# A linear-attention and feed-forward kernel: a table of engines and a new written-out order for its opening

## The chip, the cores and the metric

The kernel runs on one core of a Trainium2 chip. The metric is the device time of that core in microseconds (us). The core has a matrix engine (PE, whose weight loads are shown apart as PEld), a vector engine (DVE), a scalar engine (ACT), a general engine (POOL) and SP, whose queue issues nearly all transfers here.

## The reference

Attention over a small memory is followed by a feed-forward layer. Cut to what matters:

```python
# q, k, v: (8, 8, 576, 64); phi: (8, 8, 576, 32)
a = softmax(phi, axis=2)                       # over the 576 positions
k_m, v_m = a^T k, a^T v                        # 32 rows for each head
attn = softmax(q k_m^T / 8, axis=-1)           # over 32
x = (attn v_m), heads side by side             # (4608, 512)
h = x @ w_in                                   # w_in (512, 2048)
out = (h - tanh(h)) @ w_out                    # w_out (2048, 512)
```

## The kernel before

Every matrix operand is split into a high and a low f16 part, so one product is two or three products of f16. The weights arrive as 64-bit floats. They are loaded in 32 tiles of 512 KB, i0 to i15 of `w_in` and o0 to o15 of `w_out`. Two tiles make a pair, p = 0 to 15 (pairs 8 to 15 are of `w_out`). A pair is turned into f16 in steps: the upper bits are cast into `tops`, then joined with the lower words to f32 in `wq` or `wt`, then scaled and rounded to the high part `win_hi` or `wout_hi`, and what is left becomes `win_lo` or `wout_lo`.

The rows fall into 18 units of 256; a batch b has 576 rows, so a unit can span two batches. The hidden dimension falls into four blocks fb. For a batch, the logits `pt` are loaded and their maximum `mx` is taken, they go through the exponential, and PE turns them (`pet`, `pel`) into `e`. PE then pools keys and values with them (`pkv`), DVE normalizes the result (`kr`, `kvn`), and PE turns it (`ptr`) into `kT` and the value parts `vh`, `vl`. Scores `psc` are made for each half t of the rows; their softmax runs in place in `sc` (maximum `sm`, subtraction, exponential, sum `sz`, division), and the turned result `af` is split into `ah` and `al`. For each block, the pooled values times `w_in` (`pp`) are split into `ph` and `pl`. A first product `h` of `ah`, `al` with `ph`, `pl`, a polynomial on ACT and DVE (`u`, `h`, `g`) and a second product `o` with `w_out` finish a unit.

Units 4 to 17 run in a regular loop. Everything before it is the opening: some 180 us whose order stands as a written-out list of words, `START`. Each word advances one step by one piece: `FX0` loads the logits of batch 0, `KA0` and `KB0` its keys and values, `i4:kv2` two weight tiles into a buffer, `Q00` a half of its queries, `V00` and `V01` are the pooling, `N0` the normalization, `U0` and `UV0` the turn, `S00` the scores of half 0, `AM`, `AE`, `AD`, `AT`, `AS` the softmax and split of a half, `T01` a pair's conversion, `Lp00` its low part through PE, `P00` and `PL00` a block's `pp` with its high and its low part, `H10` the first product of unit 1 and block 0, `a` and `ap` the polynomial, `M00` the second product. `Z00` is two warming products (`warm`), whose result nobody reads. After the list `in_order` ties every engine to the order in which its instructions were written. So an engine that waits holds up all that is written behind it. SP's transfers go through the same list, and an issue waits while eight transfers are under way.

The one psum buffer `pa` serves, one after the other, `psc` of half 0, every `pp` of the opening and, from batch 1 on, `pet`, `pkv` and `ptr`. Two buffers `h` serve the first products, the low parts through PE and part of batch 0. What the change touches are the steps `top_bias`, `expo_rows`, `expo_turn`, `soft_max`, `soft_div`, `conv`, `low`, `low_pool`, `att_split`, `g2_high`, `g3`, and `START`.

Of the kernel before, what the change touches and what calls it, by code (L numbers as in the profile page):

```python
# [20 lines left out]
P = 128  # L21
# [31 lines left out]
N_ROWS = 2  # L53
# [18 lines left out]
Z00 o11:pp5 Q11 N1 Tv10 U1 Tv08 U1 Tv10 H01 o8:gg T11 UV1 UV1 T11 T09 W0 a10 ap00 Tv08 Lv09 S10 S10 ap00 H11 Lv08 H01
Tv10 a10 ap01 AM10 c00 H11 S11 Tv10 M00 a11 a10 P10 AM10 i8:kv2 c10 S11 AE10 a11 L11 AMv11 KB2 AD10 M10 AMv11 P11 a11
i10:kv3 AD10 L11 P10 Th04 AT10 AE11 a11 FA2 FX2 P11 PL10 ap01 Lv10 cv11 AS10 AD11 PL11 ap01 o10:q AD11 Tv05 Tv05
i14:kv3 M11 AT11 Tv05 Th04 ap01 cv01 Th04 OP1 AS10 AS11 H20 H20 AS11 i12:kv2 o9:q H21 ap20 Tv05 M01 Th04 ap20 H21 Lv04
a21 X2 T07 Lv05 ap20 XP2 KA2 a21 a21 ap20 H31 H30 OP0 Y2 H30 P02 P02 T07 cv20 T07 H31 Tv12 a21 Y2 c21 Tv12 T13 M20
Tv06 V20 PL02 Q20 V21 H02 T07 a31 ap30 ap30 Lv07 a31 Tv12 ap30 a31 H12 P12 Tv12 Tv06 Tv06 M21 Tv06 N2 a31 Lv06 P12 H02
T13 ap02 ap30 c30 PL12 o14:kv3 ap02 ap02 OP2 P03 o12:kv2 M30 P03 PL03 H12 Q21 U2 H03 ap12 T13 H13 ap02 W1 ap12 UV2 U2
Tb14 T13 UV2 c02 ap12 ap12 H03 Tb14 S20 Tb14 a03 H22 c31 Tb15 P13 S20 H13 ap13 L12 c12 ap13 P13 Tb14 M31 AM20 FQ3 S21
ap13 PL13 X3 H22 a03 a03 OP3 Lv13 H23 AM20 AE20 P20 H23 a03 S21 KR30 ap13 G00 AMv21 a22 R1 a22 AMv21 L12 W2 AE21 M02  # L80
Tb15 Tb15 Tb15 cv13 a22 Lv14 Lv15 M12 a23 M13 P20 a23 P21 c03 AD20 a22 PL20 H32 a23 a23 P21 AD20 H32 H33 M03 O1 cv22
AT20 ADv21 G10 AS20 PL21 H33 ADv21 a32 O1 R0 M22 AS20 a32 ap33 ap33 O0 a32 a32 FA3 P22 cv23 H41 ap33 cv32 AT21 H40 G01
O0 G20 AS21 ap33 c33 H40 M23 P23 M32 H41 P22 ap40 G21 PL22 ap40 R2 O2 P23 ap41 O2 ap40 R3 ap40 AS21 ap41 ap41 M33 PL23
ap41 c40 G11 cv41 G30 O3 F40 O3 G31
"""
W_TAG = "qt us ot qt ot qt pr ot qt pr us ot qt us ot qt".split()
N_CHECK = N_F1 + 2 * B + DF // P + DM // P


class Attention:  # L90
# [172 lines left out]
    def turn(self, b, d, ps=None):  # L263
# [9 lines left out]
        nc.scalar.activation(d["kT"], pa[:, 0, 0:128], AF.Copy)  # L273
# [29 lines left out]
    def soft_max(self, b, d, t, eng=None):  # L303
# [12 lines left out]
    def soft_div(self, b, d, t, scale, eng=None):  # L316
# [7 lines left out]
        (eng or nc.gpsimd).tensor_tensor(s3, s3, z.unsqueeze(2).to_broadcast((P, NB, 32)), op=ALU.mult)  # L324
# [971 lines left out]
```

## Time and profile before

| | us |
|---|---|
| median of 3 runs (642.98 to 643.99) | 643.63 |
| span of the profiled execution | 640.4 |
| PE busy in it | 629.1 (98%) |
| DVE busy | 515.6 (81%) |
| ACT busy | 371.7 (58%) |
| POOL busy | 233.7 (36%) |

The span is that of the instructions of one profiled execution. The median of the timed runs lies 3.2 us above it. Warming products count as busy time of PE like any others.

### The profile page before, as it was taken

The numbers are of one execution on the slowest core, as the hardware profiler recorded it, in microseconds if no ns is written. First come the engines' busy times: TensorE is split into PE (matmuls) and PEld (weight loads), VectorE is DVE, ScalarE is ACT, GpSimd is POOL, SyncE is SP. The second block draws the span as 40 slices with busy tenths as digits, with TensorE's granted clock in tenths as the row PEclk, the third lists the DMA queues.
The fourth block names the chain that finished last, engine by engine and source line by source line (L and its number), as shares of the span: only waits on it lengthen the run. The fifth ranks groups of instructions, "written<-read, shape, count | busy, mean of one in ns | idle before, by whom it ended". The sixth has DMA issues, their size and how long they took to land.

```text
span 640.4 us, 15316 instructions
## 1 busy us (share of the span) xinstructions
PE 629.1 (98%) x6592; PEld 453.4 (71%) x6592; DVE 515.6 (81%) x757; ACT 371.7 (58%) x493; POOL 233.7 (36%) x155
## 2 busy tenths in 40 slices
PE   7899999999999999999999999999999999999997
PEld 3364665645667777787777787777788777888886
DVE  3989998979785777876898889878988888858765
ACT  2878588645424455545565465545565576676641
POOL 1306212511212244422534363434432565455430
PEclk9999999999999999999999999999999999999999
DMA  8994573233122402244313422441353334234200
GB/s 333 410 401 202 194 293 136 68 120 133 53 86 104 166 5 76 39 152 174 107 58 136 173 74 69 157 175 34 108 159 140 100 105 129 62 113 131 92 35 37
DMA packets 27723, 85.48 MB, mean 133 GB/s; under 512 B 3584, under 2 KB 4096, under 8 KB 26880
## 3 DMA queue, kind: packets, MB, share of 16 engines
q1 hardware_dynamic: 26496, 82.34, 37.0%
q10 hardware_dynamic: 1152, 2.10, 0.9%
q8 instruction: 53, 0.87, 0.6%
q14 instruction: 22, 0.18, 0.1%
HBM read 72.88 MB, written 11.54 MB: 132 GB/s over the span
## 4 chain that ended last, share of the span: by engine, by line
PE 72%; DVE 9%; issue 6%; ACT 5%; POOL 4%; DMA 3%; SPq 0%; POOLq 0%; ACTq 0%; DVEq 0%
PE hs L628 17%; PE x L773 12%; PE o L766 10%; PE o L709 8%; PE o L773 8%; PE h L628 6%; PE pp L580 3%; POOL g L664 2%; PE pkv L241 2%; DVE h L653 2%; DVE h L643 2%; DMA q<-in_qt_dram 2%; ACT u L635 2%; PE o1h L709 2%; DVE f L677 2%
## 5 line engine op out<-in xcount | busy, mean ns | idle before, releaser
L664 POOL TENSOR_TENSOR g<-h,g 128x1024 f16<-128x1024 f32 x63 | 137.2, 2178 | 330.9 <-ACT g L659 244.2
L628 PEld LDWEIGHTS <-ph 128*128 128x128 f16 x2304 | 177.6, 98 | 18.5 <-issue 4.7
L628 PE MATMUL hs<-ah,ph 128*128 128x256 f16 (+3 forms) x1152 | 151.4, 246 | 0.0
L659 ACT ACTIVATE g<-h 128x1024 f16<-128x1024 f32 x72 | 76.0, 1056 | 111.6 <-DVE h L653 103.2
L628 PE MATMUL hs<-al,ph 128*128 128x256 f16 (+3 forms) x576 | 127.6, 246 | 0.0
L643 DVE SCALAR_TENSOR_TENSOR h<-hs,u 128x1024 f32<-128x1024 f32 x54 | 65.8, 1219 | 72.5 <-ACT u L635 71.8
L648 ACT ACTIVATE u<-u,beta 128x1024 f32<-128x1024 f32 x72 | 82.5, 1147 | 65.2 <-DVE h L643 65.2
L766 PE MATMUL o<-wout_hi,g 128*128 128x512 f16 x432 | 104.6, 379 | 0.0
L773 PEld LDWEIGHTS <-f 128*128 128x128 f16 x896 | 87.7, 98 | 10.2
L653 DVE SCALAR_TENSOR_TENSOR h<-u,h 128x1024 f32<-128x1024 f32 x72 | 88.7, 1233 | 4.1 <-ACT u L648 3.1
L773 PEld LDWEIGHTS <-g 128*128 128x128 f16 x672 | 64.2, 98 | 27.3 <-issue 6.0
L773 PE MATMUL x<-bt,f 128*128 128x256 f16 x672 | 82.5, 273 | 0.0
L635 ACT ACTIVATE u<-hs 128x1024 f32<-128x1024 f32 x54 | 54.8, 1014 | 27.1 <-PE hs L628 24.4
L709 PEld LDWEIGHTS <-g 128*128 128x128 f16 x384 | 36.8, 98 | 46.6 <-issue 3.3
L677 DVE TENSOR_TENSOR f<-g 128x512 f16<-128x512 f16 x112 | 68.3, 650 | 1.7
L766 PEld LDWEIGHTS <-g 128*128 128x128 f16 x432 | 41.2, 98 | 40.2 <-issue 3.8
L709 PE MATMUL o<-wout_hi,g 128*128 128x512 f16 x192 | 58.8, 380 | 0.0
L628 PE MATMUL h<-ah,ph 128*128 128x256 f16 (+3 forms) x384 | 49.6, 246 | 0.0
L628 PE MATMUL h<-al,ph 128*128 128x256 f16 (+2 forms) x192 | 42.5, 246 | 0.0
L709 PE MATMUL o<-wout_lo,g 128*128 128x512 f16 x96 | 36.4, 379 | 0.0
L598 DVE SCALAR_TENSOR_TENSOR ph<-pp,ph 128x1024 f16<-128x1024 f32 x26 | 31.5, 1211 | 3.1 <-ACT ph L593 3.1
L495 POOL TENSOR_TENSOR fy<-chk 128x512 f32<-128x512 f32 x32 | 33.6, 1064 | 0.0
(164 smaller groups left out, 936.7 us busy)
## 6 DMA issues: line engine op xcount, KB each, us to landing
q<-in_qt_dram SPq DMA_DIRECT2D x16, 576.0 KB, 5.1
kv<-in_kva_dram SPq DMA_DIRECT2D x16, 516.0 KB, 6.9
chk<-in_w_in_dram SPq DMA_DIRECT2D x16, 512.0 KB, 6.1
chk<-in_w_out_dram SPq DMA_DIRECT2D x16, 512.0 KB, 3.4
out_dram<-r SPq DMA_DIRECT2D x28, 256.0 KB, 2.4
kv<-in_kva_dram SPq DMA_DIRECT2D x6, 1032.0 KB, 9.7
raws<-in_w_in_dram SPq DMA_DIRECT2D x12, 511.8 KB, 8.9
raw<-in_w_out_dram SPq DMA_DIRECT2D x12, 511.8 KB, 9.1
```

What stands on the lines that cost most here:

```text
L495: nc.gpsimd.tensor_tensor(y, hf, hf, op=ALU.mult)
L628: nc.tensor.matmul(hp[:, k, tu : tu + w], px[:, g, cs], d[ax][:, g, ta : ta + w], start=(n == 0), stop=(n == 5),)
L635: nc.scalar.activation(uu, hp, AF.Square, scale=1.0 / (S_A * S_P))
L643: nc.vector.scalar_tensor_tensor(h3, hp, C2 * S_G / (S_A * S_P), uu, op0=ALU.mult, op1=ALU.mult)
L648: nc.scalar.activation(uu, uu, AF.Square, bias=c["beta"])
L653: nc.vector.scalar_tensor_tensor(h3, uu, CC, hp, op0=ALU.add, op1=ALU.mult)
L659: nc.scalar.activation(gg[:, 0], h3, AF.Copy)
L664: eng.tensor_tensor(gg[:, 1], h3, gg[:, 0], op=ALU.subtract)
L677: nc.vector.tensor_tensor(o, x, y, op=op)
L709: nc.tensor.matmul(o, gx[:, k, P * tt : P * tt + P], wx[:, 4 * fb + k, :], start=(first and k == 0 and wx is wout_hi and gx is gh), stop=( ...
L766: nc.tensor.matmul(o[th], gg[:, 0, k, P * th : P * th + P], wout_hi[:, 4 * fb + k, :], start=(first and k == 0), stop=False)
L773: nc.tensor.matmul(dst, a(1 - n, kk), b(n, kk), start=(new and kk == 0 and n == 0), stop=(end and kk == 1 and n == 1))
```

## The change

Three things change. `START` is written anew: the logits of batch 0 are loaded first, the loads of the weight tiles come in another order and partly in other buffers, most of the warming products move, and the pieces are interleaved differently. A table `ENGINE_LIST` names the engine (v for DVE, g for POOL, otherwise ACT or the step's default) of each copy, scaling and difference, where before a letter in the word chose it. And the two rows of logits of a batch (`pt[:, 0]`, `pt[:, 1]`) go apart through maximum, exponential and turn.

```diff
-KB0 Z00 Z00 Z00 FX0 i4:kv2 X0 Z00 Z00 KA0 Z00 Z00 YX0 Z00 Z00 i0:pp4 Z00 Z00 Z00 XT0 XT0 Z00 V00 Tv02 Tv02 V01 Tv02 N0
+FX0 Z00 XR00 XR01 YX00 KA0 XT00 YX01 XT01 KB0 XT00 V00 XT01 XT01 Z00 V01 Z00 Z00 N0 U0 Z00 i4:kv2 Q00 T02 T02 UV0
...
+ENGINE_LIST = """
+g: hi1 hi12 lo1 lo10 lo12 lo13 lo14 lo4 lo5 lo6 sc6 tops12 tops14 tops6 tops9
+v: ah11 ah21 al01 al20 al21 div01 div21 e00 el0 el1 gh0_1 gh0_2 gh0_3 gh1_2 gh2_1 gh2_3 gh3_2 gh3_3 gl0_1 gl0_3 gl1_1
+v: gl1_2 gl2_0 gl2_2 gl4_1 hi15 hi2 hi4 hi7 kT2 ph13 ph21 sub00 sub01 sub10 tops10 tops11 tops2
+"""
+ENGINES = {name: row[0] for row in ENGINE_LIST.strip().splitlines() for name in row[2:].split()}
...
+def engine_of(name, default):
+    return ENGINES.get(name, default)
+
+
+def on(nc, name, default):
+    return {"v": nc.vector, "g": nc.gpsimd}[engine_of(name, default)]
+
+
+def cast(tc, c, name, default, o, x, scale=None):
+
+    nc, e = tc.nc, engine_of(name, default)
+    if e == "a":
+        nc.scalar.activation(o, x, AF.Copy, scale=1.0 if scale is None else scale)
+    elif scale is None:
+        (nc.vector if e == "v" else nc.gpsimd).tensor_copy(o, x)
+    elif e == "v":
+        nc.vector.tensor_scalar(o, x, scale, None, op0=ALU.mult)
+    else:
+        nc.gpsimd.tensor_tensor(o, x, scale_of(c, scale, o.shape), op=ALU.mult)
...
-    def top_bias(self, b, d):
-        mx = self.big.tile([P, 2], F32, tag="mx", name=f"mx{b}")
-        self.tc.nc.vector.tensor_reduce(mx, d["pt"], axis=AX.X, op=ALU.max, negate=True)
...
+    def top_row(self, b, d, r):
+        if r == 0:
+            d["mx"] = self.big.tile([P, 2], F32, tag="mx", name=f"mx{b}")
+        self.tc.nc.vector.tensor_reduce(d["mx"][:, r : r + 1], d["pt"][:, r], axis=AX.X, op=ALU.max, negate=True)
+
+    def expo_row(self, b, d, r):
+        self.tc.nc.scalar.activation(d["pt"][:, r], d["pt"][:, r], AF.Exp, bias=d["mx"][:, r : r + 1])
+
+    def turn_row(self, b, d, r, ps, ps_tail):
...
         for c in range(4):
-            for r in range(2):
-                nc.tensor.transpose(pe[:, 2 * c + r], pt[:, r, P * c : P * c + P], self.c["ident"])
...
+            nc.tensor.transpose(pe[:, r, c], pt[:, r, P * c : P * c + P], self.c["ident"])
+        nc.tensor.matmul(pb[64 * r : 64 * r + 64, 0:P], pt[:, r, 512:S], self.c["ident"], start=True, stop=True)
+        yield
+        cast(self.tc, self.c, f"e{b}{r}", "a", d["e"][:, 0:8].rearrange("p (c r) x -> p r c x", r=2)[:, r], pe[:, r])
+        yield
+        if r:
+            cast(self.tc, self.c, f"el{b}", "a", d["e"][:, 8], pb[:, 0:P])
...
-        (eng or nc.gpsimd).tensor_tensor(s3, s3, m.unsqueeze(2).to_broadcast((P, NB, 32)), op=ALU.subtract)
+        on(nc, f"sub{b}{t}", "g").tensor_tensor(s3, s3, m.unsqueeze(2).to_broadcast((P, NB, 32)), op=ALU.subtract)
...
     def low(p):
-        lo = low_of(p)
+        lo, shared = low_of(p), engine_of(f"lo{p}", "v") == "g"
+        if shared:
+            for i in range(2):
+                cast(tc, c, f"sc{p}", "a", tfs[p][i], tfs[p][i], S_W)
+        yield
         for i in range(2):
-            nc.vector.scalar_tensor_tensor(
-                lo[:, i], tfs[p][i], S_W, his[p][:, i], op0=ALU.mult, op1=ALU.subtract
-            )
+            if shared:
+                on(nc, f"lo{p}", "v").tensor_tensor(lo[:, i], tfs[p][i], his[p][:, i], op=ALU.subtract)
+            else:
+                nc.vector.scalar_tensor_tensor(lo[:, i], tfs[p][i], S_W, his[p][:, i], op0=ALU.mult, op1=ALU.subtract)
```

Of `START`, 26 words `Z00` become 19, which is 52 and 38 warming products. Before the first turn of logits there are 24 of them before and 2 after. Between the scores of half 0 and half 1 of batch 0 there are 2 before and 22 after.

On PE, at the pooling of batch 0. `pet0` and `pel0` are the turned logits, `pkv00` the pooled product. Before:

```order
L871 LDWEIGHTS nid16_66
L871 MATMUL warm_110<-nid16_66 128x512
L241 MATMUL pkv00_167<-kv00_128,e0_162 32x129 x16
L241 MATMUL pkv00_167<-kv01_108,e0_162 32x129 x16
L249 MATMUL pkv00_167<-kt0_130,e0_162 32x129 x8
L269 MATMUL ptr0_224<-ident_58,kvn0_216 128x128 x2
```

After, the first half of the pooling follows the turned logits, and a warming pair stands between its halves:

```order
L256 MATMUL pet0_120<-ident_58,pt0_107 128x128 x4
L257 MATMUL pel0_121<-ident_58,pt0_107 64x128
L276 MATMUL pkv00_137<-kv00_116,e0_122 32x129 x16
L888 LDWEIGHTS nid16_65
L888 MATMUL warm_109<-nid16_65 128x512
```

The pooling moved up against the turn of the logits, and the warming pair went from in front of it to its middle.

On ACT, where the tiles i0 to i3 are cast and the scores of batch 0 go through the exponential (`sc0`). Before:

```order
L414 ACTIVATE tops1_106<-raw0_142 128x512
L414 ACTIVATE tops1_106<-raw1_218 128x512
L273 ACTIVATE kT0_232<-ptr0_224 128x128
L457 ACTIVATE win_hi_100<-wt20_185 128x512
L457 ACTIVATE win_hi_100<-wt21_186 128x512
L457 ACTIVATE win_hi_100<-wq0_227 128x512 x2
L314 ACTIVATE sc0_251<-sc0_251 128x576
L414 ACTIVATE tops0_104<-raw2_236 128x512
L414 ACTIVATE tops0_104<-raw3_240 128x512
```

After:

```order
L107 ACTIVATE tops0_103<-raw2_215 128x512
L107 ACTIVATE tops0_103<-raw3_218 128x512
L349 ACTIVATE sc0_229<-sc0_229 128x576
L107 ACTIVATE win_hi_99<-wq0_261 128x512 x2
L107 ACTIVATE wq1_281<-wq1_281 128x512 x2
L107 ACTIVATE tops1_105<-raws6_238 128x1024
L107 ACTIVATE win_lo_100<-pw0_303 128x2x512
L349 ACTIVATE sc0_229<-sc0_229 128x576
```

The casts of i2 and i3 now stand ahead of the first exponential, and a scaling of pair 1 (`wq1`) stands between it and the casts of i6 and i7.

On POOL, behind its clearing of `tops`. Before:

```order
L311 TENSOR_TENSOR sc0_251<-sc0_251,sm00_266 128x576
L311 TENSOR_TENSOR sc0_251<-sc0_251,sm01_276 128x576
L324 TENSOR_TENSOR sc0_251<-sc0_251,sz01_307 128x576
L571 TENSOR_TENSOR al0_386<-af0_322,ah0_385 128x2x288 x2
L664 TENSOR_TENSOR g00_647<-h300_630,g00_647 128x1024
```

After:

```order
L113 TENSOR_TENSOR win_hi_99<-wq1_281,sw_64 128x512 x2
L359 TENSOR_TENSOR sc0_229<-sc0_229,sz00_284 128x576
L504 TENSOR_TENSOR win_lo_100<-wq1_281,win_hi_99 128x512 x2
L597 TENSOR_TENSOR al0_342<-af0_321,ah0_341 128x2x288
L109 CAST tops0_103<-raw18_279 128x512
```

The two subtractions of the softmax left POOL, and the high and the low part of pair 1 came to it, on either side of the division of half 0.

## Rows read from the trace of the kernel before

**Rows 1.** The page: engine, busy us (share) xinstructions; granted clock in tenths.

```profile
PE 629.1 (98%) x6592; PEld 453.4 (71%) x6592; DVE 515.6 (81%) x757; ACT 371.7 (58%) x493; POOL 233.7 (36%) x155
...
PEclk9999999999999999999999999999999999999999
```

**Rows 2.** Windows: from:to length, busy of PE, PEld, DVE, ACT, POOL; clock, DMA.

```profile
200.00:640.00 440.00, 435.90 (x4726) 340.16 (x4723) 349.09 (x539) 249.39 (x331) 180.31 (x114) 1.00 0.31 103
```

**Rows 3.** Timeline of PE: start, length, line, operation, count [idle before, released by].

```profile
3.47 8.13 PE L871 MATMUL warm<-nid 128*128 128x512 f16 x24 [3.47 <-DVE nid L1239]
11.44 1.04 PE L221 MATMUL pet<-ident,pt 128*128 128x128 f32 x8
...
13.59 1.98 PE L241 MATMUL pkv<-kv,e 128*32 128x129 f32 x64 [0.21 <-ACT e L226]
...
16.93 0.44 PE L269 MATMUL ptr<-ident,kvn 128*128 128x128 f32 x2 [0.98 <-DVE kvn L257]
...
32.67 0.27 PE L628 MATMUL h<-ah,ph 128*128 128x256 f16 x1
...
43.23 0.60 PE L871 MATMUL warm<-nid 128*128 128x512 f16 x2
44.37 0.41 PE L269 MATMUL ptr<-ident,kvn 128*128 128x128 f32 x2 [0.54 <-DVE kvn L257]
...
51.35 0.39 PE L709 MATMUL o<-wout_hi,g 128*128 128x512 f16 x1
```

**Rows 4.** Timeline of PE's weight loads, the last slow one and the next.

```profile
8.57 0.15 PEld L871 LDWEIGHTS <-nid 128*128 128x128 f16 x1 [0.28 <-issue]
8.99 2.11 PEld L871 LDWEIGHTS <-nid 128*128 128x128 f16 x10 [0.28 <-issue]
```

**Rows 5.** Chain that ended last, two of its pieces: start, length, what.

```profile
1.18 6.04 DMA pt<-in_phx_dram
...
7.24 11.87 DMA q<-in_qt_dram
```

**Rows 6.** Timeline of DVE, opening.

```profile
7.24 1.35 DVE L207 TENSOR_REDUCE mx<-pt 128x2 f32<-128x1152 f32 x1 [3.63 <-DMA pt<-in_phx_dram]
...
23.38 1.22 DVE L422 SCALAR_TENSOR_TENSOR wq<-raw,tops 128x512 uint32<-128x512 uint32 x2
...
26.42 0.78 DVE L329 STREAM_TRANSPOSE af<-sc 128x576 f32<-128x576 f32 x1
...
31.01 1.22 DVE L598 SCALAR_TENSOR_TENSOR ph<-pp,ph 128x1024 f16<-128x1024 f32 x1
...
37.35 1.23 DVE L598 SCALAR_TENSOR_TENSOR ph<-pp,ph 128x1024 f16<-128x1024 f32 x1 [2.00 <-ACT ph L593]
...
47.35 1.29 DVE L470 SCALAR_TENSOR_TENSOR wout_lo<-wt,wout_hi 128x512 f16<-128x512 f32 x2
...
58.41 2.17 DVE L653 SCALAR_TENSOR_TENSOR h<-u,h 128x1024 f32<-128x1024 f32 x1
```

**Rows 7.** Timeline of ACT, opening.

```profile
8.63 1.44 ACT L212 ACTIVATE pt<-pt,mx 128x576 f32<-128x576 f32 x2
...
22.07 1.39 ACT L414 ACTIVATE tops<-raw 128x512 f16<-128x512 bf16 x2
...
24.95 1.14 ACT L457 ACTIVATE win_hi<-wq 128x512 f16<-128x512 f32 x2
...
36.30 1.02 ACT L593 ACTIVATE ph<-pp 128x1024 f16<-128x1024 f32 x1 [0.53 <-PE pp L580]
```

**Rows 8.** Timeline of POOL, opening.

```profile
20.29 1.16 POOL L311 TENSOR_TENSOR sc<-sc,sm 128x576 f32<-128x576 f32 x1 [16.96 <-DVE sm L309]
...
25.92 1.47 POOL L324 TENSOR_TENSOR sc<-sc,sz 128x576 f32<-128x576 f32 x1 [3.00 <-DVE sz L322]
...
59.47 3.25 POOL L489 TENSOR_TENSOR wout_lo<-wt,wout_hi 128x512 f16<-128x512 f32 x2
```

**Rows 9.** Waits of PE after 50 us: us in total, times, longest.

```profile
PE pmx L173 <- DVE dg L160: 0.6, 1, 0.6
```

More of the change, by code (lines that the diff above doesn't have):

```diff
@@ L52 @@
 N_F1 = 32
-N_ROWS = 2
 P_TAG = {}
@@ L72 @@
[L72 to L76, printed above, removed]
@@ L90, with scale_of @@
+def scale_of(c, scale, shape):
+    x = c["sw"]
+    for _ in shape[2:]:
+        x = x.unsqueeze(1)
+    return x.to_broadcast(tuple(shape))
 class Attention:
@@ new lines, in expo_row @@
+    def expo_row(self, b, d, r):
+        self.tc.nc.scalar.activation(d["pt"][:, r], d["pt"][:, r], AF.Exp, bias=d["mx"][:, r : r + 1])
+    def turn_row(self, b, d, r, ps, ps_tail):
+        nc, pt = self.tc.nc, d["pt"]
+        if r == 0:
+            d["pe"] = self.psum(f"pet{b}", ps).rearrange("p a x -> p (a x)").rearrange("p (r c x) -> p r c x", r=2, x=P)
+            d["pl"] = ps_tail.tile([P, 512], F32, tag="o1", name=f"pel{b}")
+            d["e"] = self.big.tile([P, 9, 128], F32, tag="e", name=f"e{b}", bufs=1)
+        pe, pb = d["pe"], d["pl"]
@@ L272, in turn @@
         d["kT"] = self.big.tile([P, 128], F32, tag="kT", name=f"kT{b}", bufs=1)
-        nc.scalar.activation(d["kT"], pa[:, 0, 0:128], AF.Copy)
+        cast(self.tc, self.c, f"kT{b}", "a", d["kT"], pa[:, 0, 0:128])
     def scores(self, b, d, t, ps=None):
@@ L410, in to_tops @@
             o, x = y[:, n * i : n * i + n, 1], r.bitcast(BF16).rearrange("p (f w) -> p f w", w=4)[:, :, 2]
-            if dve:
-                nc.vector.tensor_copy(o, x)
-            else:
-                nc.scalar.activation(o, x, AF.Copy)
+            cast(tc, c, f"tops{p}", "a", o, x)
     def to_f32(p, y, ts):
@@ L453, in conv @@
         for o, x in todo:
-            if form in ("h", "b"):
-                nc.vector.tensor_scalar(o, x, S_W, None, op0=ALU.mult)
-            else:
-                nc.scalar.activation(o, x, AF.Copy, scale=S_W)
+            cast(tc, c, f"hi{p}", "a", o, x, S_W)
     def half_of(p, win, wout):
@@ L480, in low_pe @@
         yield
-        nc.scalar.activation(lo, pw, AF.Copy)
-    def low_pool(p):
-        lo = low_of(p)
-        for i in range(2):
-            nc.scalar.activation(tfs[p][i], tfs[p][i], AF.Copy, scale=S_W)
-        yield
-        for i in range(2):
-            nc.gpsimd.tensor_tensor(lo[:, i], tfs[p][i], his[p][:, i], op=ALU.subtract)
+        cast(tc, c, f"pw{p}", "a", lo, pw)
     def window(k):
@@ L551, in att_turn_v @@
         d["p"] = [None] * NFB
-        nc.scalar.activation(d["vh"], pv, AF.Copy, scale=S_V)
+        cast(tc, c, f"vh{b}", "a", d["vh"], pv, S_V)
         yield
@@ L592, in att_p @@
         sc = S_P / (S_V * S_W)
-        nc.scalar.activation(ph, pa, AF.Copy, scale=sc)
+        cast(tc, c, f"ph{b}{fb}", "a", ph, pa, sc)
         d["p"][fb] = (ph, pl, pa)
@@ L598, in att_pl @@
         nc.vector.scalar_tensor_tensor(pl, pa, S_P / (S_V * S_W), ph, op0=ALU.mult, op1=ALU.subtract)
-    def att_pl_pe(b, fb):
-        ph, pl, pa = st[b]["p"][fb]
-        p_terms(b, fb, pa, False)
-        for g in range(2):
-            nc.tensor.matmul(pa[:, g], c["nidp"], ph[:, g], start=False, stop=True)
-        yield
-        nc.scalar.activation(pl, pa, AF.Copy, scale=S_P / (S_V * S_W))
     def segs(u):
@@ L1055, in split_path @@
         g2_high(u, fb)
-        g3(u, fb, nc.vector if (u, fb) == slots[-1] else nc.gpsimd)
+        g3(u, fb, nc.vector if (u, fb) == slots[-1] else None)
         while due and due[0][0] == "C":
```

83 lines of the change are left out of this document (37 added, 46 removed).

## The prediction

> **What bounds the kernel now.** I read the page first, then the windows after the opening, then PE's timeline of the first 52 us with the timelines of the engines that feed it. On the page PE is busy for 629.1 of 640.4 us [rows 1]. From 200 us to the end it works 435.90 of 440 us [rows 2]: the regular loop is bound by PE, and the change does not touch it. The opening decides, and there busy time misleads, since warming products count. What PE loses stands in its timeline [rows 3]: 3.47 us before anything, 24 warming products until 11.6, gaps ahead of the turn of batch 0, and later two warming pairs of 0.6 us and a gap of 0.54 before the turn of batch 1 at 44.37. From there to 640 us PE lacks work only for 0.6 us ahead of `pmx` [rows 9] and the 4.1 us of rows 2. Useful products are the same before and after. So the change is worth what it moves the moment from which PE is full, plus what stalls it adds later.
>
> Three other things feed the opening. Transfers run in issue order at a steady rate: the logits land at 7.22 us, behind the keys and values of row 1 (1032 + 576 KB, by the tiles' shapes), and the second half of the queries at 19.11, when 6098 KB are in [rows 5]. That is 4490 KB in 11.89 us, 378 KB per us, with a start at 3.0 us. DVE and ACT are nearly full from 20 us on.
>
> **The clock.** The page says full speed throughout [rows 1], but the weight loads of the first warming products stand 0.42 us apart up to 8.99 and ten of them then take 2.11 us [rows 4]. For 512 columns that is the low level (1.2 GHz) and then the high one (2.4 GHz). PE had been working without a break since 3.47 [rows 3], so it rose 5.5 us after its first product.
>
> **The new order, step by step.** I follow the chain of the new order with durations of the old one.
>
> 1. Logits first: 576 KB land at 3.0 + 1.5 = 4.5 us instead of 7.22. Maximum by rows (1.35 together, [rows 6]) and exponentials (0.72 each, [rows 7], the table load hidden as before) end at 7.4 instead of 10.07.
> 2. Only one warming pair stands ahead, so PE is slow when it turns the logits. Eight turns take 1.04 us at the high level [rows 3], twice that here: 6.75 to 9.4. Keys and values land at 7.3 and 10.7. The pooling (1.98 and some 0.45 us for the last rows, [rows 3]) starts at 9.4; its first half takes 1.9 at the low level, a warming pair 0.86. If the clock has risen by its second half, at about 12.2, pooling ends at 13.7. If not, at 14.95. Before: 15.9.
> 3. Normalizing and turning take 1.4 us as before [rows 3]. Scores of half 0 start at 15.7, against 17.8; their queries land at 14.9 by the rate of rows 5.
> 4. DVE then has pair 2 to join (cast and two joins, 2.0 us), so the turned scores are ready at 17.65, the maximum and the subtraction, now on DVE instead of POOL's 1.16 us [rows 8], at 19.05.
> 5. Here the gain stops. ACT holds the exponential behind the casts of i2 and i3. By the rate, i3 lands at 20.3 (3.0 + 6546 / 378), the casts (0.7 each, [rows 7]) end at 21.1, and the exponential at 21.8. Pair 1 is joined at 22.4 instead of 24.6 [rows 6].
> 6. Pair 1 then goes to POOL: high part, division of half 0, low part. No row shows POOL scaling a tile by a broadcast. Its differences bound it: 1.16 for 576 elements [rows 8] and 1.62 for 512 when DVE reads two inputs from SBUF beside it (3.25 for two, [rows 8]). I take 1.2, nearest to the undisturbed rows. The high part ends at 24.1, the division at 25.4, the turned half 0 at 26.5 instead of 27.2 [rows 6], the low part at 27.8.
> 7. ACT's scaling of pair 1 waits for POOL's high part, and the casts of i6 and i7, the low part of pair 0, the second exponential, the high part of pair 3 and `ah` wait behind it. With their rows' durations (0.57 for a scaled tile, 1.02 for a `pp`, [rows 7]; the others alike by their sizes) the high part of `pp` 00 comes at 31.6, its low part on DVE at 32.8, half a microsecond later than before (32.2, [rows 6]). The low part of pair 3 comes at 33.6; `pp` 01 waits for it. Both first products of block 0 (2.7 us each) end at 39.4. Before, with the same `pp` inside, they ended at 38.8.
> 8. Batch 1: its second low part of `pp`, maximum and one step of the polynomial keep DVE busy until 39.4 (37.35 + 1.23 was the low part's end before, [rows 6]; now 36.75). ACT then squares (1.1), and only behind that copies `e` by rows until 41.7. Pooling shares the buffer `pa` with the turned logits, so it runs from 41.7 to 44.1. Before, PE had done the same work and waited until 44.37 [rows 3]. Now the next first product stands right behind the pooling and fills the wait. Gain: 0.3.
> 9. From 35 to 50 DVE's list holds 14.2 us of work without a break (eight full blocks or pairs at 1.2, as 37.35 and 23.38 in rows 6, and 4.6 us of smaller steps), and PE's scores of batch 1 wait for its `vl`, at about 50.2, when PE arrives at 49.8. So 0.4 is lost. The second product starts at 50.85. Before: 51.35, less 0.65 for the scores of half 1, which now come later, 50.70 [rows 3]. Net so far: 0.15 later.
> 10. `pmx` now stands behind a second product of 5.3 us, and `dg` is ready by then: the 0.6 us of rows 9 goes. I add 0.25 for reads of DVE that POOL slows, as in 58.41, where 2.17 stands for a step that takes 1.2 [rows 6].
>
> The sum is 0.15 − 0.6 + 0.25 = −0.2 us. On the profiled execution that is 640.4 − 0.2 = 640.2. The median stands 3.2 us above that execution's span, so 643.4. The pieces after 60 us change places too, but PE was full there with DVE nearly full; the counts of DVE's steps nearly balance (eight casts of `g` come, twelve low parts of weights go), so I take nothing for them.
>
> *A rule speaks against step 6: the Trainium skill ("GPSIMD Engine Reference", 4.1 Engine selection) sends elementwise work on tiles to the vector engine and calls POOL about twice as slow for two inputs. The trace is worse: 1.62 [rows 8] against DVE's 0.65 for the same difference (1.29 for two, [rows 6]). By the page's factor a tile would cost 1.3, which adds 0.2 to the sum.*
>
> **The rivals.**
>
> *The cover works better than I think (faster).* If step 8's copies of `e` and step 9's `vl` come in time, PE loses nothing between 38.8 and 44.4, where it lost two pairs of 0.6 and a gap of 0.54 [rows 3], less one new pair of 0.43: 1.3 us, and the 0.6 of rows 9. That is 640.4 − 1.9 = 638.5, or 641.7. For it: DVE's second low part is 1.8 us ahead in my sum. Against it: one ACT queue stands between.
>
> *The clock stays low (slower).* It decides at 12.2 us. If PE is still at 1.2 GHz when the second half of the pooling starts, steps 2 to 4 lose 1.2 us, pair 1 is joined at 23.5 and everything behind follows: 643.4 + 1.2 = 644.6. If it is low through the scores too, the 22 warming products behind them cost 0.43 instead of 0.21 each, and the second half's scores and the low part of pair 0 behind them slip: I take 2.8 us, 646.2. For it: before, the rise took 5.5 us of gapless full products [rows 4], and here the work from 6.75 on is turns and narrow products. Against it: from 6.75 PE has no gap either. *The Trainium skill ("TensorE: Matmul & The Clock Gate", Part 1, What's actually happening) says that the throttled state is the default and that activity releases it. By that rule the change, which takes 22 products away at the front, begins lower for longer; rows 4 agree on the default, and when the clock rises here no row shows.*
>
> *POOL is dear.* At 1.62 for each of its tiles the two parts of pair 1 take 6.5 instead of 4.8 us, and ACT's scaling waits 0.9 longer. Half of that is covered by the chain of step 8; with the casts of o2 and o3, for which no row shows a price, I take 1.2 later: 644.6.
>
> **How the numbers follow.** About 0.2% (1.3 us) is what a measurement of this kernel can tell from no change. My forecast, 643.4, has a chance of 0.46, the better cover 0.20 (641.7), the low clock 0.22 (644.6 to 646.2), dear POOL 0.12 (644.6). Faster by over 1.3 us, below 642.3: the better cover and a little of the forecast's own spread, 0.24. Slower, above 644.9: two thirds of the low clock, 0.14, half of dear POOL, 0.06, and a little of the forecast, 0.06, together 0.26. The rest, 0.50, is the same. The range is 641.2 to 646.2, the better cover with 0.5 to spare, and the low clock's far end.
>
> **What the next profile would show.** Step 1: `mx` starts at 4.5 on DVE. Step 2: the weight loads of the 22 warming products stand 0.21 apart from the first. Step 5: the exponential on ACT starts right behind the cast of i3, near 21.1. Step 6: POOL's two rows of `win_hi` take about 2.4. Step 8: `pkv` of batch 1 starts near 41.7, released by ACT's `e`. Step 10: no wait of PE for `dg`. The prediction is wrong if PE after 60 us waits over 1 us in sum, or if the first product of block 0 does not start within 1 us of 34.1.

## The result: 0.8% slower, 649.5 us

The changed kernel takes 649.48 us (median of 4 runs, 647.75 to 650.55), the kernel before 643.66 beside it. The ratio is 1.0083 with a 95% interval of 1.0070 to 1.0095. I had forecast 643.4, no difference, with a range up to 646.2, so forecast and range are both wrong. The profiled execution has a span of 646.0 us where the kernel before had 640.4: 5.6 us to explain. Times and spans scatter between executions by more than before, and I come back to that.

The page of the changed kernel: engine, busy us (share) xinstructions, then the granted clock in tenths over 40 slices. They answer to [rows 1].

```profile
PE 628.1 (97%) x6578; PEld 453.3 (70%) x6578; DVE 523.1 (81%) x760; ACT 364.1 (56%) x484; POOL 260.5 (40%) x177
...
PEclk9999998999999999999999999999999999999999
```

TensorE (PE) does the same work, POOL (GpSimd) 27 us more, and one slice, the seventh, has a lower clock. The waits of PE over the whole span say where to look (line waited for, us in total, times, longest):

```profile
PE ptr L304 <- DVE kvn L292: 2.1, 1, 2.1
PE pkv L276 <- DVE ph L624: 2.0, 1, 2.0
...
PE h L645 <- DVE h L660: 0.6, 1, 0.6
```

The list leaves out the waits before 23 us, of 3.5, 2.3 and 1.5 us, since the first products of block 0 came as early as forecast. Before, PE waited at `ptr` as well, 0.98 us in batch 0 and 0.54 here [rows 3]; the other two waits are new. The 0.6 us for `pmx` of [rows 9] is gone (0.4 of it was back in a later profile of the same kernel). **The first stall** lies where batch 1 is turned. PE's timeline around it, to set against [rows 3]:

```profile
41.55 1.98 PE L276 MATMUL pkv<-kv,e 128*32 128x129 f32 x64 [0.27 <-ACT e L107]
43.47 0.45 PE L284 MATMUL pkv<-kt,e 64*32 64x129 f32 x16
...
48.70 0.41 PE L304 MATMUL ptr<-ident,kvn 128*128 128x128 f32 x2 [2.06 <-DVE kvn L292]
49.74 0.27 PE L645 MATMUL h<-ah,ph 128*128 128x256 f16 x1 [0.63 <-DVE h L660]
...
53.10 0.39 PE L726 MATMUL o<-wout_hi,g 128*128 128x512 f16 x1
```

What VectorE (DVE) did meanwhile, and POOL beside it:

```profile
43.92 0.80 DVE L109 CAST tops<-raw 128x512 f16<-128x512 bf16 x2 [1.03 <-DMA raw<-in_w_out_dram]
44.61 3.21 DVE L454 SCALAR_TENSOR_TENSOR wq<-raw,tops 128x512 uint32<-128x512 uint32 x2
47.75 0.15 DVE L289 TENSOR_SCALAR kr<-pkv 128x2 f32<-128x2 f32 x1
...
48.13 0.42 DVE L292 TENSOR_TENSOR kvn<-pkv,kr 128x256 f32<-128x256 f32 x1
...
52.01 0.29 DVE L580 SCALAR_TENSOR_TENSOR vl<-ptr,vh 128x128 f16<-128x128 f32 x1
...
44.60 2.68 POOL L681 TENSOR_TENSOR g<-h,g 128x1024 f16<-128x1024 f32 x1 [8.51 <-ACT g L107]
```

The pooling ended at 43.9, but `kvn` ran at 48.1. Ahead of it in DVE's list stand the casts and joins of weight pair 10 (o4 and o5). DVE waits 1.03 us for o4's transfer, and the two joins take 3.21 us where the same form took 1.22 before [rows 6], while POOL makes `g`. Before, `kvn` stood ahead of that pair, and PE's `ptr` followed at 44.37 [rows 3].

**The second stall** lies at 99 to 101 us. ACT, DVE, POOL, then PE:

```profile
93.84 0.79 ACT L107 ACTIVATE tops<-raw 128x512 f16<-128x512 bf16 x1 [2.85 <-DMA raw<-in_w_out_dram]
...
94.66 1.59 DVE L454 SCALAR_TENSOR_TENSOR wq<-raw,tops 128x512 uint32<-128x512 uint32 x1 [2.94 <-ACT tops L107]
...
99.87 1.22 DVE L624 SCALAR_TENSOR_TENSOR ph<-pp,ph 128x1024 f16<-128x1024 f32 x1
...
...
93.66 2.04 POOL L113 TENSOR_TENSOR wout_hi<-wq,sw 128x512 f16<-128x512 f32 x2
...
101.14 2.50 PE L276 MATMUL pkv<-kv,e 128*32 128x129 f32 x64 [2.00 <-DVE ph L624]
```

Again a tile comes late: o11's load is issued at 87.78, behind a load that waits for a buffer until 86.25. Its join takes 1.59 us beside POOL's `wout_hi`; in the run below with `gl0_0` on DVE it takes 0.69, and PE still waits 2.16 us there, so the late tile decides. After the idle stretch the clock falls, as the windows show (from:to length, PE busy, granted clock, DMA share, GB/s); 64 pooling products take 2.50 us, not 1.98:

```profile
100.00:102.00 2.00, 0.86 (x32) 1.00 0.01 4
102.00:104.00 2.00, 2.00 (x59) 0.61 0.04 8
104.00:106.00 2.00, 2.00 (x25) 0.54 0.00 0
106.00:108.00 2.00, 2.00 (x33) 1.00 0.00 0
```

Two windows of 2 us at 0.61 and 0.54 lose 0.78 + 0.92 = 1.7 us. My account of the 5.6: the first product of block 0 into the output starts at 53.10, not 51.35, and the scores of the second half, 0.65, now stand behind it: 2.4 later. Less 0.6 for `pmx`, plus 2.0 and 1.7 for the second stall: 5.5.

### The profile page after: what moved, and what is told of

Same layout as the page of the kernel before. It is cut to its first block, busy times and chain, and to the rows that moved or that the text cites. A ratio compares the mean times of both kernels' runs of the same rounds, so it can differ in the third digit from the quotient of the medians.

```text
span 646.0 us, 15313 instructions
## 1 busy us (share of the span) xinstructions
PE 628.1 (97%) x6578; PEld 453.3 (70%) x6578; DVE 523.1 (81%) x760; ACT 364.1 (56%) x484; POOL 260.5 (40%) x177
## 4 chain that ended last, share of the span: by engine, by line
PE 71%; DVE 7%; issue 6%; DMA 5%; ACT 5%; POOL 4%; SPq 1%; POOLq 0%; ACTq 0%; DVEq 0%
PE hs L645 16%; PE x L790 12%; PE o L783 10%; PE o L726 8%; PE o L790 8%; PE h L645 6%; PE o1h L726 3%; PE pp L606 3%; DMA raw<-in_w_out_dram 2%; DMA raw<-in_w_in_dram 2%; PE pkv L276 2%; POOL g L681 2%; ACT u L652 2%; DVE h L660 2%; DVE h L670 2%
## 5 line engine op out<-in xcount | busy, mean ns | idle before, releaser
L681 POOL TENSOR_TENSOR g<-h,g 128x1024 f16<-128x1024 f32 x64 | 140.0, 2188 | 327.1 <-ACT g L107 202.6
L107 ACT ACTIVATE g<-h 128x1024 f16<-128x1024 f32 x64 | 67.6, 1056 | 104.7 <-DVE h L670 101.4
L790 PEld LDWEIGHTS <-f 128*128 128x128 f16 x896 | 87.6, 98 | 10.2
L783 PEld LDWEIGHTS <-g 128*128 128x128 f16 x432 | 41.2, 98 | 40.2 <-issue 3.8
```

The source lines that it names most:

```text
L107: nc.scalar.activation(o, x, AF.Copy, scale=1.0 if scale is None else scale)
L681: (eng or on(nc, f"gl{u}_{fb}", "g")).tensor_tensor(gg[:, 1], h3, gg[:, 0], op=ALU.subtract)
L783: nc.tensor.matmul(o[th], gg[:, 0, k, P * th : P * th + P], wout_hi[:, 4 * fb + k, :], start=(first and k == 0), stop=False)
L790: nc.tensor.matmul(dst, a(1 - n, kk), b(n, kk), start=(new and kk == 0 and n == 0), stop=(end and kk == 1 and n == 1))
```

## The experiments

Theory A: a load that lands late holds DVE's list, and what PE needs stands behind it. Rivals: the collision of POOL and DVE (C), the clock (F, L), and a loss spread over the whole new order (E). Every edit below is of the changed kernel's order or table, if no other is named. Weight tiles are i0 to i15 and o0 to o15; `T10`, `N1`, `a10` and so on are words of the order.

**Once more, and with the gap filled.** The changed kernel beside the next run:

> The changed kernel itself, once more, on the chip of the three runs that follow, so that each has its base beside it. Expected 648 to 650.5 us, with a mean granted clock of 0.994 to 0.997; where the mean is lower, the time is longer by about 0.0035 x 640 / 0.003 = roughly 2 us for each 0.003, since each fall of the clock for some 3 us to half costs about that.

It took 648.49 us (ratio 1.0075, 1.0058 to 1.0093). (The product in the expectation is written wrongly: 0.003 x 640 is 1.9 us, which agrees with its 2 us.) The clock's mean was 0.994 to 0.997 in its four executions. In this profile the fall stood behind the first stall: window 50 to 52 us at 0.50. Then four warming pairs in the first gap:

```diff
- H01 T10 T09 N1 L09 U1
+ H01 T10 T09 N1 L09 Z00 Z00 Z00 Z00 U1
```

> The changed kernel with four more pairs of warming products (some 1.7 us of work without a use) ahead of the ptr transposes of the second batch, where TensorE otherwise idles for 2.06 us; no wait is shortened. Theory F (part of the loss is the clock, which falls after such an idle stretch in some executions and not in others): with the gap filled the granted clock stays at 1.00 between 48 and 56 us in every execution, only the fall behind the second gap at 101 us is left, and the time is 646.5 to 648.5, less scattered. Theory G (the clock's fall has another cause, and the wait itself is the loss): the time is that of the changed kernel or up to 0.5 us longer, since the products may end after the wait.

It took 645.88 us (ratio 1.0026, 1.0016 to 1.0037), 2.6 less, with a mean clock of 1.00 in all ten executions. `kvn` came no earlier:

```profile
47.68 1.89 PE L887 MATMUL warm<-nid 128*128 128x512 f16 x8
49.78 0.41 PE L303 MATMUL ptr<-ident,kvn 128*128 128x128 f32 x2 [0.21 <-DVE kvn L291]
50.82 0.27 PE L644 MATMUL h<-ah,ph 128*128 128x256 f16 x1 [0.63 <-DVE h L659]
```

As theory F has it, useless products give back 2.6 us though `kvn` is no earlier. The fall that theory F left behind the second stall came in none of the ten executions either. The wait there was 1.0 us in this profile, where the two profiles without the fill had 2.0 and 1.8; why no fall followed is not shown. About half of the loss goes with the clock behind the stalls.

**The other way round.** In the kernel before, `kvn` and the first steps of the turn (`N1`, `U1`) went behind the steps of weight pair 10, and one of pair 8:

```diff
- N1 Tv10 U1 Tv08 U1 Tv10 H01
+ Tv10 Tv08 Tv10 N1 U1 U1 H01
```

> The kernel before with one edit, the other way round: the second batch's norm product kvn goes behind tile 10's cast and join on VectorE, as it stands in the changed kernel. There GpSimd is idle beside the join, which takes 1.28 us and the casts 0.79, with the tile loaded by then. Theory A (the place of kvn behind that tile costs what stands ahead of it): the wait at ptr grows from 0.54 by about 1.9 us, and the granted clock falls behind it in some executions: 644.1 + 1.9 to 644.1 + 4, that is 645.5 to 648. Theory C (it is the contention, not the place): below 645, since TensorE has the first unit's products to run elsewhere.

It took 648.19 us (ratio 1.0056, 1.0039 to 1.0073). The wait of 0.54 [rows 3] became 2.16 (PE's timeline), and the clock fell to 0.50 behind it:

```profile
46.29 0.41 PE L268 MATMUL ptr<-ident,kvn 128*128 128x128 f32 x2 [2.16 <-DVE kvn L256]
```

The window behind it (columns as above):

```profile
48.00:50.00 2.00, 2.00 (x11) 0.50 1.05 428
```

This one edit makes the kernel before nearly as slow as the changed one, though its joins there take an undisturbed 1.28 us, with POOL idle. The place alone is enough for such a loss; part of it shows later, as the wait for `pmx` is 1.8 us and not 0.6.

**`kvn` back to the front** in the changed kernel:

```diff
- T11 T10 T08 Q10 ap00 H10 V11 Q20 H01 T10 T09 N1 L09
+ T11 T08 Q10 ap00 H10 V11 N1 Q20 T10 H01 T10 T09 L09
```

(The first `T10` goes behind `Q20` as well.)

> The changed kernel with one word moved: the keys' norm product of the second batch (kvn on VectorE) goes ahead of both halves of the cast and join of weight tile 10, in place of behind them. Theory A (a tile whose load lands late holds VectorE's row, and kvn stands behind it): TensorE's wait of 2.06 us at ptr goes, the wait of 0.63 us at the h matmuls may stay, since its copy still stands behind the join; the time falls by 1.5 to 2.7 us against the changed kernel, to 646.8 to 648.0. Theory B (the loss is the slower granted clock and the contention of GpSimd with VectorE, not the order): kvn is early but the same work is late elsewhere, and the time stays within 0.5 us of 649.5. The second stall at 99 to 101 us stays under both.

It took 648.77 us (ratio 1.0082, 1.0060 to 1.0105), so nothing is gained. The wait at `ptr` went, and a longer one came right behind it (timelines of PE and DVE):

```profile
50.70 0.27 PE L644 MATMUL h<-ah,ph 128*128 128x256 f16 x1 [2.88 <-DVE h L659]
...
45.72 2.62 DVE L108 CAST tops<-raw 128x512 f16<-128x512 bf16 x2
48.23 1.28 DVE L453 SCALAR_TENSOR_TENSOR wq<-raw,tops 128x512 uint32<-128x512 uint32 x2
49.43 1.21 DVE L659 SCALAR_TENSOR_TENSOR h<-h,u 128x1024 f32<-128x1024 f32 x1
```

The pair's casts now fall beside POOL's `g` and take 2.62 instead of 0.80, and the gated step `h` behind them is as late as `kvn` was. Theory A named the late pair rightly, but missed the second step that stands behind it.

**The collision taken away.** The low half of `g` goes from POOL to DVE:

```diff
- v: ah11 ah21 al01 ... tops11 tops2
+ v: ah11 ah21 al01 ... tops11 tops2 gl0_0
```

> The changed kernel with one entry added to the engine table: the copy g of the low half of h00 is made by VectorE instead of GpSimd, so that GpSimd is idle while VectorE joins weight tile 10 (3.21 us beside the copy, 1.28 us for the same form in other places). Theory C (GpSimd's copy slows VectorE's join by sharing its way into the memory): the join falls to 1.3 to 1.6 us, TensorE's wait at ptr from 2.06 to 0 to 0.5 us if the copy itself, some 1.2 us on VectorE, comes behind the join, and the time falls by 0.5 to 1.9 us. Theory D (the join is long of itself there, for instance since its raw tile is still landing): the join stays near 3.2 us, and the time stays the same or rises by the 1.2 us of the copy.

The joins fall from 3.21 to 1.29 us, in the same place and on the same data (timelines of DVE and PE):

```profile
44.42 1.29 DVE L453 SCALAR_TENSOR_TENSOR wq<-raw,tops 128x512 uint32<-128x512 uint32 x2
...
46.58 0.41 PE L303 MATMUL ptr<-ident,kvn 128*128 128x128 f32 x2 [0.17 <-DVE kvn L291]
...
50.98 0.39 PE L725 MATMUL o<-wout_hi,g 128*128 128x512 f16 x1
```

The time is 646.63 us (ratio 1.0040, 1.0026 to 1.0053), 1.9 less. PE's wait at `ptr` is nearly gone, and the second product starts at 50.98 instead of 53.10; the prediction had 50.85. So two things add up at the first stall: the place behind a late pair, and POOL beside it.

**The second stall.** o11's load ahead of the one that waits:

```diff
- H31 o14:kv3 T06 ... a21 o11:sc L07
+ H31 o11:sc o14:kv3 T06 ... a21 L07
```

> The changed kernel with one load moved: the load of weight tile 11 of the out matrix is issued ahead of the load of tiles 14 and 15, which waits for a buffer until 86.25 us; nothing else moves. Theory A (late load): the stall of 2.0 us ahead of pkv at 101 us goes, and with it the fall of the granted clock to 0.5 to 0.7 between 102 and 106 us, which cost about 1.75 us more; the time falls by 3.0 to 4.0 us to 645.5 to 646.5. Theory B (the clock falls there for another cause than the gap, say the pattern of weight loads): only the 2.0 us go, to 647.5, and the window 102 to 106 us still shows 0.5 to 0.7. If the tile was not the last to come (VectorE is behind by its own work), less than 1 us goes.

It took 646.25 us (ratio 1.0043, 1.0027 to 1.0058), 2.2 less than the changed kernel's 648.49 and 3.2 less than its 649.48; the stall at 101 us and the fall of the clock behind it are gone from the profile. But in this profile the clock fell behind the first stall (0.75, 0.50 and 0.90 from 48 to 54 us), where it had stayed up in the first. What was won at one gap was in part lost at the other.

**All three moves**: `kvn` and o11's load as above, and o4's load ahead of the second batch's logits.

```diff
- AS00 FX1 Z00 ... PL01 o4:pp5 T11
+ AS00 o4:pp5 FX1 Z00 ... PL01 T11
```

> The changed kernel with three words moved at once: kvn of the second batch ahead of tile 10's cast and join, the load of out tiles 4 and 5 before the first forward pieces instead of behind eight others, and the load of out tile 11 ahead of that of 14 and 15. Theory A (both stalls come from late loads and nothing else is lost): waits of 2.06, 0.63 and 2.0 us and the 1.75 us of low clock go, 649.5 - 6.4 = 643.1, range 642 to 644.5, the same as the kernel before or a little faster. Theory E (the new order is slower in many small places and the two stalls are only where the loss shows up): the time stays above 646, and TensorE's busy time from 200 us on differs from before.

The median is 646.97 us (ratio 1.0053, 1.0034 to 1.0072), so theory A's 643.1 was missed. One execution, with a mean clock of 1.00, took 644.04; the other four, at 0.997, 646.3 to 647.2. The wait left over is the `h` of the run with `kvn` alone, 2.79 us here. I then moved what I took for that step:

```diff
- N1 Q20 T10 H01 T10 T09 L09
+ N1 Q20 H01 T10 T10 T09 L09
```

> The kernel with all three moves, but with the norm product kvn and also the gated step h of the first unit's second quarter (H01) ahead of tile 10's cast and join on VectorE; there the run with three moves still waited 2.79 us, for that step behind a cast of 2.53 and a join of 1.28 us. Theory A (what stands behind the late tile on VectorE decides): that wait falls to 1.0 to 1.3 us (the copy itself, 1.22 us from 46.4 on), and the idle stretch is too short to bring the clock down, so that the mean granted clock is 0.999 to 1.0: 644.0 - 1.6 = 642.4, range 641.5 to 643.5, faster than the kernel before by 0.1 to 0.3%. Theory E (the new order loses elsewhere too): not under 644.

It took 647.22 us (1.0047, 1.0034 to 1.0061). `H01` is PE's products, not DVE's step; the wait stayed at 2.57. With three warming pairs in the gap:

```diff
- L09 U1 L11
+ L09 Z00 Z00 Z00 U1 L11
```

> The kernel of the run before with three pairs of warming products ahead of the ptr transposes of the second batch. They take about 1.3 us of TensorE, in a stretch where it is expected to wait 1.0 to 1.3 us anyway, but ahead of ptr and not behind it. If the gap brings the clock down in some executions, they pay: the same lowest time, and fewer long ones. If the gap is harmless, they cost 0.3 to 1.3 us. Expected 642 to 644.

it is 644.50 us (1.0008, 0.9997 to 1.0018), all twelve executions at 0.999 or 1.00; without the pairs, six of seven stood at 0.996 or 0.997. This is the clock again, 2.7 us, at an unchanged order of DVE.

**The right word.** The gated step is the first word `a10`:

```diff
- N1 Q20 H01 T10 T10 T09 L09 U1 L11 L08 a10 L09
+ N1 Q20 H01 a10 T10 T10 T09 L09 U1 L11 L08 L09
```

> The kernel with all three moves and kvn ahead, with one more word moved: the first word of the gated chain of unit 1's first quarter (VectorE's step h at line 659) goes ahead of tile 10's cast and join; the word H01 moved in an earlier run was the products, not this step. Its inputs are there by 45.2 us (ScalarE's u), so it should run from 45.3 to 46.4, ahead of the end of the ptr transposes at 46.7. Theory A (VectorE's row behind the late tile is the whole of the first stall): the wait of 2.6 us falls under 0.5, the granted clock is 1.00 in every execution, and the time is 641 to 642.5 us, faster than the kernel before by 0.2 to 0.5%. Theory E (the new order loses in other places too): 643.5 or more although that wait is gone.

It took 643.71 us (ratio 0.9997, 0.9988 to 1.0006): level with the kernel before, 4.8 to 5.8 us under the changed one. The waits at `ptr` and `h` are gone, the casts take 0.79 and the joins 1.27. The pair now runs behind POOL's `g`, which ends at 47.7, so the move takes the collision away as well. But it is not the 642 of theory A: the next thing behind the joins, `vl`, now makes PE wait (PE's timeline):

```profile
52.19 0.72 PE L315 MATMUL psc<-q,kT 64*32 64x288 f32 x16 [1.71 <-DVE vl L579]
```

Moving the turn's words forward took two runs, since the first moved only the high half `vh`:

```diff
- a10 T10 T10 T09 L09 U1 L11 L08 L09 UV1 Q11
+ a10 T10 U1 UV1 T10 T09 L09 L11 L08 L09 Q11
```

> The kernel with three loads and words moved (o4 and o11 early, kvn and the gated step ahead of tile 10) and now also the turn of the second batch's keys and values, with vl, ahead of tile 10's join and the three low halves of weight tiles on VectorE. Theory A (what stands behind the late tile decides): the wait of 1.71 us for vl ahead of the second batch's scores goes, or comes down to 0.4 us, and the time is 643.7 - 1.5 = 642.2, range 641.5 to 643, faster than the kernel before by 0.2 to 0.35%. Theory E (the wait passes to the next thing on VectorE, the low halves that the first out products need): 643 to 644, no difference from the kernel before.

643.47 us (0.9995, 0.9986 to 1.0004), the wait unchanged at 1.71. With `vl`, the second `UV1`, too:

```diff
- a10 T10 U1 UV1 T10 T09 ... H11 H11 i14:kv3 UV1 L11
+ a10 T10 U1 UV1 UV1 T10 T09 ... H11 H11 i14:kv3 L11
```

> The kernel with o4 and o11 early, kvn and the gated step ahead of tile 10, and now vl itself ahead of tile 10's join and the three low halves. Theory A (what stands behind the late tile on VectorE decides): vl runs at 47.4 and not at 51.0 us, the scores of the second batch follow the h matmuls at 49.6 us without a wait, and 1.7 us go: 643.5 - 1.6 = 641.9, range 641.2 to 642.7, faster than the kernel before by 0.2 to 0.4%. Theory E (the wait passes on to the low halves that the next out products need): 643 to 643.7.

643.40 us (0.9997, 0.9988 to 1.0006). The wait for `vl` is gone, and the time is the same. PE now waits further on (its timeline):

```profile
57.62 0.72 PE L315 MATMUL psc<-q,kT 64*32 64x288 f32 x16 [0.70 <-DVE sc L324]
58.73 0.38 PE L725 MATMUL o1h<-wout_hi,g 128*128 128x512 f16 x1 [0.39 <-DVE h L659]
```

Theory E is right about the time. The profile shows 1.1 of the 1.7 us again, as waits for the next steps in DVE's list. The rest it can't tell: in it the pooling of batch 1 started at 42.56, in the profile of the run before at 41.68.

**The table apart from the order.** The changed order with the engines of before:

```diff
- g: hi1 hi12 lo1 lo10 lo12 ... tops6 tops9
+ g: lo11 lo12
- v: ah11 ah21 al01 al20 ... tops2
+ v: tops2 tops8 tops10 ... gl3_2 gl4_1
```

> The changed kernel's order with the engines of the kernel before in the table (GpSimd has two entries in place of fifteen, VectorE twenty-four in place of thirty-eight). Theory C (GpSimd beside VectorE is the loss): VectorE's join of tile 10 takes 1.3 us and not 3.2, the wait at ptr falls from 2.06 to 0.3 us or less, and the time falls by 2 us or more to 644 to 646.5. Theory A (the order and the late loads are the loss, whichever engine does the copies): VectorE, with more of its own work ahead, is as late or later, and the time is 648 to 652.

It took 668.87 us (1.0393, 1.0372 to 1.0414), far beyond every expectation. PE waits 4.1 us for `win_lo` at `pp` and 4.3 for `vl`, 3.4 for a gated step, and 1.2 to 1.7 at five more places (line waited for, us in total, times, longest):

```profile
PE psc L315 <- DVE vl L579: 4.5, 2, 4.3
PE pp L605 <- DVE win_lo L505: 4.1, 2, 2.8
...
PE h L644 <- DVE h L659: 3.4, 1, 3.4
```

So this order needs POOL's larger share. What the share costs shows in its collisions with DVE and in `lo1`, below.

**What is left at the opening.** PE waits 0.5 to 1.3 us near 29.4 for the low part of pair 1, POOL's `lo1`, which takes 3.77 us for two tiles. (The profile names DVE's `sz` as the releaser, which `pp` does not read; `lo1` ends in the same 0.1 us.) The division ahead of it moved to DVE, in the kernel with `vh` moved:

```diff
- v: ah11 ah21 al01 ... tops11 tops2
+ v: ah11 ah21 al01 ... tops11 tops2 div00
```

> The kernel of the run beside it, with the division of the first batch's softmax by VectorE (some 0.76 us) in place of GpSimd (1.15 us), where it stands between the high halves and the low halves of weight tile 1. Theory A (GpSimd's row of hi, division, lo is late for the pp products): the low halves end 1.1 us earlier and TensorE's wait of 0.5 to 1.3 us at pp goes, 0.3 to 1.0 us faster than the run beside it. Theory H (VectorE is the engine that decides there): its row is 0.76 us longer, the second tile's exponential and the a factors come later, and the time is the same or 0.3 to 0.8 us longer.

644.56 us (1.0016, 1.0007 to 1.0025), 1.1 us more than the run beside it, above theory H's 0.8. PE's wait for the low part did go, as theory A has it. But the division took DVE 1.24 us beside POOL, not 0.76, and PE waited 0.6, 0.3 and 0.9 us for later steps of DVE: it has no room there, as theory H has it. Last, the idle stretch from 4.5 to 6.8 us was filled with two warming pairs, all but 0.5 us of it, in the kernel with `vl` moved and in the changed kernel:

```diff
- FX0 Z00 XR00 XR01
+ FX0 Z00 Z00 Z00 XR00 XR01
```

> The best kernel so far (643.4 us) with two more pairs of warming products right behind the first pair, at 4.5 to 6.6 us, where TensorE otherwise waits 2.3 us for the first exponential. Theory L (the low clock at the front costs): the first pooling products take 1.1 us and not 1.95 in the profiled execution, GpSimd's high halves of tile 1 begin at 22.0 and not 23.1 us, and the first h products at 33.3 and not 34.6: 642.0 to 642.8, 0.6 to 1.3 us faster than without, and 0.2 to 0.3% faster than the kernel before. Rival M (what is won at the front is lost again in waits for the loads and for VectorE): 643.2 to 643.6, no difference.

643.46 us (1.0000, 0.9991 to 1.0009), no difference. The fill did not do what it was for: the first pooling products still ran at the low level, 1.95 us for 32.

> The changed kernel with the same two pairs of warming products and nothing else. Theory L: 0.3 to 1.3 us faster, 647.5 to 648.5, since the two stalls at 47 and 100 us stay as they are. Rival M, and the prediction on record, which put the low clock at the front at no more than 1.2 to 2.8 us with a chance of 0.22: no difference, 648.3 to 649.5.

647.41 us (1.0055, 1.0040 to 1.0070); its interval overlaps that of the changed kernel (1.0058 to 1.0093), so this tells nothing. A kernel with the order and the engines of before and only the row-by-row opening gave no time, so what that opening does by itself is open. No version beats the kernel before by more than the measurement can tell.

## Why the prediction was wrong

**Steps 1 to 8 came out.** DVE's maximum, ACT's exponential (the sign for step 5) and POOL's high part (step 6), then DVE's turned half 0:

```profile
4.59 1.41 DVE L242 TENSOR_REDUCE mx<-pt 128x1 f32<-128x576 f32 x2 [1.08 <-DMA pt<-in_phx_dram]
...
21.67 0.66 ACT L349 ACTIVATE sc<-sc 128x576 f32<-128x576 f32 x1
...
22.16 2.34 POOL L113 TENSOR_TENSOR win_hi<-wq,sw 128x512 f16<-128x512 f32 x2 [18.79 <-DVE wq L454]
...
26.15 0.77 DVE L364 STREAM_TRANSPOSE af<-sc 128x576 f32<-128x576 f32 x1
```

Forecast were 4.5 for the maximum, about 21.1 for the exponential's start, 2.4 us for POOL's two tiles, 26.5 for the turned half (it ended at 26.9). The scores of half 0 started at 15.34 (15.7 forecast), the first products of block 0 at 33.58 (34.1 give or take 1), the pooling of batch 1 at 41.55 (41.7), released by ACT's `e`. Only POOL's low part took 3.77 us where I had 2.4; that cost PE 0.59. Step 2 came out partly by luck: the turns took until 10.2 and not 9.4, but the clock had risen by then in this execution (the first half of the pooling took 1.09 us, not 1.9), so the pooling ended at 13.4, where I had 13.7.

**Step 9 failed.** I took DVE's list from 35 to 50 us as work without a break at undisturbed durations, which put `vl` at 50.2, and let PE lose 0.4 us there and nothing ahead of it. `vl` came at 52.01, but PE had lost its time before: 2.06 us at `ptr` for `kvn` and 0.63 at `h`, two waits that the step does not have. DVE's list has a break of 1.03 us, since o4's load lands late: I had used the transfer rate for i2 and i3 only, and not for the later tiles. And one of its joins takes 2.62 us. Step 10's 0.25 for reads that POOL slows was the term for that; one collision alone cost 1.9. At the first stall this was the term most out of size: with that collision gone, the second product starts 0.13 us from where step 9 had put it, though o4 is as late (1.05 us).

**"The pieces after 60 us ... I take nothing"** failed by 3.7 us. I counted DVE's steps and found them balanced; what decided was one load behind another that waits for a buffer: 2.0 us of waiting and 1.7 of low clock, both gone from the profile with o11's load moved. The test I had named, over 1 us of waiting after 60 us, did show it.

**The rivals.** The low clock was right in kind and wrong in place. I priced it for the opening, where it does vary between executions (the first 32 pooling products in 1.09 or 1.95 us). Where the second 32 were slow as well (1.52 us in the run with `vl` moved), the pooling of batch 1 started at 42.56 and not at 41.2 to 41.8. That is about 1 us, near the 1.2 of the rival; how much of it reaches the end is not shown. The clock's larger cost struck behind the stalls, as gaps of 2.0 to 2.9 us were followed by 0.5 in some executions and not in others; that I had no rival for. Dear POOL was right for `lo1`, and its collisions with DVE were worth more than its own slowness. With two loads, `kvn` and the gated step moved, the order takes 643.4 to 643.7 us, close to what the sum said. Several moves lie between the two, so this agreement does not prove every term. What was missing was the order on DVE behind late loads, and the price of a collision with POOL.

## What to carry to other kernels

When an order is rewritten, follow each load to the first instruction that needs it, and look at what stands behind that instruction on its engine: what PE needs next must not stand behind a tile that has not landed. Removing the wait that a profile names is seldom enough; the next word in the same list takes its place, so move all that PE needs or leave the list alone. For a step of DVE beside a POOL instruction, count with a delay of up to about that instruction's length, not with a slightly lower speed. An idle stretch of 2 us on PE cost nearly twice its length here (2.0 of waiting and 1.7 of low clock), and where it can't be removed some useless products in it are worth trying: they gave back 2.6 us here.

## What the runs showed of the hardware

**Beside POOL, one step of DVE waits; the steps do not all run slower.** The two joins beside `g` are not both slow. One tile's group, min/median/max in ns, in the changed kernel:

```profile
L454 DVE SCALAR_TENSOR_TENSOR wq<-raw,tops x2: 681/1650/2620, 44.6 to 45.2; 128x512 uint32<-128x512 uint32 x2
```

The casts of the run with `kvn` moved alone:

```profile
L108 DVE CAST tops<-raw x2: 436/1361/2286, 45.7 to 47.9; 128x512 f16<-128x512 bf16 x2
```

One of each pair has its usual length (681, 436) and the other is longer by 1.9 us, nearly a whole `g` (2.13 us in the second run). In the changed kernel `g` started with the first join and took 2.68 us itself; the second join was the long one. In the second profile of that kernel `g` started ahead, and the first join was the long one (POOL, then DVE):

```profile
44.76 2.16 POOL L681 TENSOR_TENSOR g<-h,g 128x1024 f16<-128x1024 f32 x1 [8.51 <-ACT g L107]
...
44.86 2.61 DVE L454 SCALAR_TENSOR_TENSOR wq<-raw,tops 128x512 uint32<-128x512 uint32 x1
```

So the two engines look as if they took turns. The Trainium skill ("SBUF — State Buffer", Who interferes with whom) says that a vector instruction with two inputs in SBUF (the on-chip memory) and a GpSimd instruction that reads SBUF exclude each other for a whole instruction; casts it names too, in a mode that uses both ports. For the joins the trace agrees, by the 2620 beside 681; in which mode these casts ran no row shows. A term "reads slowed a little" had the wrong shape: here the price was nothing for one step and 1.9 us for the other, by the order of arrival. Smaller prices occur too, as for the division above (1.24 for 0.76).

**The same gap has two prices.** In two profiles of the changed kernel the gap of 2.1 us at 47 us was followed once by a granted clock of 1.00 and once by 0.50 (windows of the first profile, then of the second: PE busy, granted clock, DMA share, GB/s):

```profile
50.00:52.00 2.00, 2.00 (x21) 1.00 0.55 207
...
50.00:52.00 2.00, 2.00 (x10) 0.50 0.55 212
```

In the run with all three moves a mean clock of 1.00 goes with 644.0 us, and 0.997 with 646.3 to 647.2. A single profile of such a kernel does not tell what it usually does.
